# A transformer block's forward and backward pass on one core: chunks emitted as a skewed pipeline, weight-gradient matmuls interleaved, broadcasts in parts over two DMA queues

## The chip, the core and the metric

The kernel runs on 1 core of one Trainium2 chip. The metric is device time in microseconds (us). TensorE (PE, with its weight loads as PEld), VectorE (DVE), ScalarE (ACT) and GpSimd (POOL) compute; SyncE (SP) and POOL each issue DMAs. Every engine works through its own list of instructions in a fixed order and waits at the first one whose inputs or buffers are not ready.

## The reference

`reference` returns the output of one block and the gradients of a given `grad_out` with respect to seven of its inputs. S = 2048 tokens, D = 512, F = 1792, 32 heads of 16, bfloat16. The attention of a token sees 8 positions: itself and 7 earlier ones, two apart.

```python
qkv = (x @ wqkv)...                         # q, k, v: heads of 16
idx = pos[:, None] - arange(8) * 2          # a window of W = 8, dilation 2
logits = einsum("bhsd,bhswd->bhsw", q, k[idx]) * scale
o = einsum("bhsw,bhswd->bhsd", softmax(logits), v[idx]) @ wo
h  = x + attention(layernorm(x))
h2 = h + gelu(layernorm(h) @ w1 + b1) @ w2 + b2
outputs: h2, and d/d(x, wqkv, wo, w1, b1, w2, b2) of sum(h2 * grad_out)
```

## The kernel before, in words

The tokens are cut into NC = 4 chunks of CH = 512 (tiles of 128 tokens by 512 features). Channels stand on the partitions, 128 at a time (G = 4 groups). The work runs in four stages.

**Forward, chunk after chunk (the loop at L227).** Layernorm, transposes and q, k, v (`psq`, L251). For each group g DVE multiplies q by eight shifted views of k (`pr`, L260) and PE sums over a head with a small indicator matrix (`lg`, L264). Softmax on DVE and ACT gives `attn` (L269 to L279), which is transposed (`pta`, `aT`) and written to DRAM by `put_wh` (`attn_f`, `attn_b`). Then `bcast` (L145) reads 1 MB back for each group, each head's row copied to its 16 channels (`bc`, L305, on SP's queue); DVE multiplies it by the shifted v (L306) and PE sums the eight products (`pso`, L309). After that come `psh` (L317), the second layernorm, the first FFN matmul (`psf`, L333), the gelu on ACT and DVE, stores of its three intermediates to `x_d`, `s_d`, `g_d` on POOL's queue, and the second FFN matmul (`ps2`, L351).

**FFN backward, chunks 3, 2, 1, 0 (`ffn_bwd`, L423).** `psg` (L447), the gelu's derivative on DVE, `psx` (L459), and the layernorm's backward (`ln_bwd`, L409), which leaves `gh`.

**Weight gradients, in two blocks.** L566 to L582 make w2's (`psw2`, L578) from `g_d`, read back through transposing DMAs on SP's queue (`gtm`, L575). `tail_weights` (L600) makes w1's and wo's (`psw1`, L612; `pswo`, L623) from `h1tm` and `otm`, read in the same way. Both are written under `later(LOW)`, which gives them a low priority in the list that the framework orders before the run; how they then lie in each engine's order is shown below.

**Attention backward, chunks 3 to 0.** `attn_bwd1` (L468): `psgo`, the product of go and shifted v (`bp`, L489) and its sums (`ga`, L493). `attn_bwd2` (L499): the softmax's backward, `put_wh` of its result to `gl_b`, then four broadcasts of `attn_b` (`bv`, L534) and four of `gl_b` (`bg`, L539), all on POOL's queue, each multiplied on DVE (L535, L541, L542) and summed on PE (`psa`, L525), then `psy` (L552) and `ln_bwd`. After all chunks the last block makes wqkv's gradient (`psq`, L653).

What orders the work: the framework emits in the order of the program text and by priority; tiles of one tag share a number of buffers, and an instruction that needs a buffer waits for its last reader. In PSUM there are 4 accumulators of one tag (`acc`, L91), 2 for transposes and 2 for `lg` and `ga`. In SBUF `pr`/`bp` and the broadcasts share the tag `big` with 4 buffers.

Of the kernel before, what the change touches and what calls it, by code (L numbers as in the profile page):

```python
# [10 lines left out]
P = 128  # L11
# [23 lines left out]
def kernel(  # L35
# [37 lines left out]
    @contextmanager  # L73
    def later(n):
        keep = tc.cur_priority
        tc.cur_priority = keep + n
        yield
        tc.cur_priority = keep

# [7 lines left out]
    ps_acc = ctx.enter_context(tc.tile_pool(name="ps_acc", bufs=4, space=PSUM))  # L87
    ps_t = ctx.enter_context(tc.tile_pool(name="ps_t", bufs=2, space=PSUM))
    ps_l = ctx.enter_context(tc.tile_pool(name="ps_l", bufs=2, space=PSUM))

    def acc(name):  # L91
        return ps_acc.tile([P, CH], F32, name=name, tag="acc")
# [70 lines left out]

    def load_x(c):
        x = fr.tile([P, TC, D], BF16, name=f"x{c}", tag="x", bufs=2)
        sync.dma_start(out=x[:], in_=tm(xf[c * CH:(c + 1) * CH, :]))
        return x

    xs = {0: load_x(0)}
    wn = A_wqkv.rearrange("(dc p) j -> p dc j", p=P)  # L170
    for dc in range(DC):
        nat = fr.tile([P, 3 * D], BF16, name=f"nat{dc}", tag="nat", bufs=2)
# [15 lines left out]
    ptb = ps_t.tile([P, 8 * P], BF16, name="ptb", tag="pt")  # L188
    nc.tensor.transpose(ptb[:, 0:FT], b1r[:, :], ident[0:FT, 0:FT])
    nc.vector.tensor_copy(out=b1c[:], in_=ptb[:, 0:FT])  # L190
    pq.dma_start(out=w1[:], in_=B_w1.rearrange("(dc p) f -> p dc f", p=P))
# [10 lines left out]
    def layernorm(src, dst, rstd, c, nm):  # L202
        st = fl.tile([P, TC, 6], F32, name=f"st{nm}", tag="st", bufs=2)
        mv = fl.tile([P, TC, 2], F32, name=f"mv{nm}", tag="mv", bufs=2)
        ve = fl.tile([P, TC], F32, name=f"ve{nm}", tag="ve", bufs=2)
# [10 lines left out]
    def to_T(src, dst, nm):  # L216
        for d2 in range(DC // 2):
            pt = ps_t.tile([P, 8 * P], BF16, name=f"pt{nm}{d2}", tag="pt")
# [7 lines left out]
    ks, vs = {}, {}  # L226
    for c in range(NC):  # L227
        x = xs.pop(c)
        if c + 1 < NC:
            xs[c + 1] = load_x(c + 1)  # L230
        ln1 = fr.tile([P, TC, D], BF16, name=f"ln1_{c}", tag="ln1", bufs=1)
        layernorm(x, ln1, rstd1, c, f"a{c}")
        pq.dma_start(out=tm(ln1_d[c][:]), in_=ln1[:])
        ln1T = fr.tile([P, DC, CH], BF16, name=f"ln1T{c}", tag="ln1T", bufs=1)
        to_T(ln1, ln1T, f"a{c}")
# [8 lines left out]
        ks[c], vs[c] = k, v  # L244
# [37 lines left out]
        def to_wh(src, sb_pool, nm):  # L282
            t_ = sb_pool.tile([P, 2, CH], BF16, name=f"aT{nm}", tag="aT", bufs=2)
            pt = ps_t.tile([P, 8 * P], BF16, name=f"pt{nm}", tag="pt")
            for b in range(2):
                for j in range(TC):
                    nc.tensor.transpose(pt[:, (b * TC + j) * P:(b * TC + j + 1) * P], src[:, j, b * P:(b + 1) * P], ident[:])
# [401 lines left out]
```

## Time and profile before

| what | us |
|---|---|
| three runs | 1167.06, 1156.75, 1151.91 |
| median | 1156.75 |
| the profiled execution | 1156.15 |
| its span, first to last instruction | 1154.4 |
| what lies around the span | 1.75 |

The profile page gives busy time by engine, then groups of instructions by line: `x16 | 36.7, 2292 | 93.1 <-DMA` means 16 instructions, 36.7 us busy, 2292 ns for one, and 93.1 us in which their engine stood idle before them, ended by that DMA. A row of the stage view has the stretch, its length, busy us of PE, PEld, DVE, ACT and POOL with the number of instructions, then the granted clock of PE (1.00 is full), the mean busy share of the 16 DMA engines, and GB/s. DMA share times length is called DMA time below; it can pass 1.0 where packets of two queues overlap on an engine.

### The profile page before, as it was taken

Reading aid. Unit: us, or ns where it says so; the run is one execution under the profiler, and the core shown is the slowest. Engines: PE = TensorE matmul, PEld = TensorE weight load, DVE = VectorE, ACT = ScalarE, POOL = GpSimd, SP = SyncE. Lnnn points to the kernel's source line nnn. Section 1 sums busy time; section 2 is a strip of 40 time slices with the busy share of each in tenths; the row PEclk is TensorE's granted clock in tenths of the full one; section 3 lists DMA queues with packets and bytes.
Section 4 is the critical chain, followed back from the end, with each engine's and each line's share of the span. In section 5 each row is a group of like instructions: output and inputs, shape, how many; then the busy total and the mean of one; then the engine's idle time right before and its main releaser. Section 6 shows DMA issues by size and latency. Waiting matters only on the chain.

```text
span 1154.4 us, 10992 instructions
## 1 busy us (share of the span) xinstructions
PE 748.9 (65%) x4066; PEld 328.0 (28%) x4066; DVE 539.5 (47%) x790; ACT 372.0 (32%) x529; POOL 270.6 (23%) x392
## 2 busy tenths in 40 slices
PE   3357844791687275788669566199784766854668
PEld 1223421340233021233224222045332232321223
DVE  3545153543445233799998500000466675585500
ACT  4117530661284045455553011011231122221201
POOL 5205330431151125434431000200212212211100
PEclk9678876895798687887999799599996786967879
DMA  7265427444452789856543844996739668577293
GB/s 263 89 143 179 159 74 159 141 164 106 104 201 92 173 170 314 245 173 182 167 144 81 185 110 107 264 189 135 186 111 221 151 165 193 150 180 197 59 229 97
DMA packets 166516, 186.18 MB, mean 161 GB/s; under 512 B 124925, under 2 KB 138110, under 8 KB 160318
## 3 DMA queue, kind: packets, MB, share of 16 engines
q0 software_dynamic: 33792, 125.95, 38.4%
q1 hardware_dynamic: 132670, 59.53, 23.6%
q8 instruction: 32, 0.52, 0.2%
q14 instruction: 22, 0.18, 0.0%
HBM read 93.00 MB, written 63.56 MB: 136 GB/s over the span
## 4 chain that ended last, share of the span: by engine, by line
issue 24%; DVE 16%; PE 12%; DMA 10%; ACT 5%; POOL 3%; SPq 1%; POOLq 0%; ACTq 0%; DVEq 0%
PE psq L653 3%; PE psa L525 2%; DMA bg<-gl_b 2%; DMA bv<-attn_b 2%; DVE gh L449 2%; DVE bp L489 2%; DMA bc<-attn_f 2%; DVE by L441 1%; PE ps L351 1%; SPq L648 1%; ACT by L435 1%; DVE by L439 1%; ACT bu L438 1%; POOL gq_d L530 1%; DVE lua L420 1%
## 5 line engine op out<-in xcount | busy, mean ns | idle before, releaser
L541 DVE TENSOR_TENSOR bh<-bg,bk 128x4096 bf16<-128x4096 bf16 x16 | 36.7, 2292 | 194.9 <-DMA bg<-gl_b 194.9
L309 PE MATMUL pso<-bc,ident 128*128 128x512 bf16 x128 | 45.0, 516 | 92.6 <-DVE bc L306 92.6
L447 PE MATMUL psg<-goutT,w2T 128*128 128x512 bf16 x224 | 63.7, 441 | 34.4 <-DVE gb1p L449 29.3
L306 DVE TENSOR_TENSOR bc<-bc,v 128x4096 bf16<-128x4096 bf16 x16 | 36.7, 2292 | 93.1 <-DMA bc<-attn_f 93.1
L578 PE MATMUL psw<-gout,gtm 128*128 128x512 bf16 x224 | 57.4, 389 | 30.3 <-DMA gtm<-g_d 30.1
L525 PEld LDWEIGHTS <-ident 128*128 128x128 bf16 x384 | 41.8, 113 | 122.5 <-issue 40.0
L333 PE MATMUL psf<-ln2T,w 128*128 128x512 bf16 x224 | 60.7, 429 | 20.3 <-ACT u L335 18.1
L612 PE MATMUL psw<-h1tm,ln2a 128*128 128x512 bf16 (+1 forms) x256 | 50.5, 359 | 25.7 <-DMA h1tm<-gh_d 25.7
L351 PE MATMUL ps<-w,g 128*128 128x512 bf16 x224 | 55.6, 397 | 11.3 <-ACT u L335 9.7
L260 DVE TENSOR_TENSOR pr<-q,k 128x4096 bf16<-128x4096 bf16 x16 | 35.8, 2296 | 56.2 <-ACT q L253 56.2
L525 PE MATMUL psa<-bh,ident 128*128 128x512 bf16 x128 | 43.2, 499 | 28.6 <-DVE bh L541 28.6
L653 PE MATMUL psq<-gqt,ln1a 128*128 128x512 bf16 x192 | 45.2, 398 | 18.9 <-DMA ln1a<-ln_d 17.6
L525 PE MATMUL psa<-bv,ident 128*128 128x512 bf16 x128 | 39.8, 475 | 23.5 <-DVE bv L535 23.5
L530 POOL DMA_DIRECT2D gq_d<-gt x48 | 25.6, 534 | 121.2 <-ACT gt L527 76.9
L459 PE MATMUL psx<-w1T,gh 128*128 128x512 bf16 x224 | 51.5, 390 | 2.3 <-DVE gb1p L449 2.3
L535 DVE TENSOR_TENSOR bv<-bv,go 128x4224 bf16<-128x4224 bf16 x16 | 37.4, 2356 | 32.5 <-DMA bv<-attn_b 32.5
L310 ACT CAST oT<-pso 128x512 bf16<-128x512 f32 x16 | 9.4, 585 | 126.5 <-PE pso L309 126.5
L309 PEld LDWEIGHTS <-ident 128*128 128x128 bf16 x128 | 14.1, 121 | 121.4 <-DVE bc L306 102.1
L527 ACT ACTIVATE gt<-psa 128x512 bf16<-128x512 f32 x32 | 19.1, 597 | 87.6 <-PE psa L525 82.7
L251 PE MATMUL psq<-ln1T,wqkv 128*128 128x512 bf16 x192 | 44.5, 394 | 0.7 <-ACT ln1T L224 0.7
L447 PEld LDWEIGHTS <-w2T 128*128 128x128 bf16 x224 | 24.4, 109 | 71.3 <-issue 53.3
L435 ACT ACTIVATE by<-bu 128x1024 bf16<-128x1024 bf16 x28 | 29.5, 1056 | 45.7 <-DVE gb1p L449 45.7
(183 smaller groups left out, 1461.6 us busy)
## 6 DMA issues: line engine op xcount, KB each, us to landing
bv<-attn_b POOLq DMA_DIRECT2D x16, 1056.0 KB, 10.6
bg<-gl_b POOLq DMA_DIRECT2D x16, 1056.0 KB, 8.5
bc<-attn_f SPq DMA_DIRECT2D x16, 1024.0 KB, 11.2
x_d<-u POOLq DMA_DIRECT2D x28, 256.0 KB, 3.4
s_d<-s POOLq DMA_DIRECT2D x28, 256.0 KB, 3.0
g_d<-g POOLq DMA_DIRECT2D x28, 256.0 KB, 3.2
bu<-x_d POOLq DMA_DIRECT2D x28, 256.0 KB, 3.2
bs<-s_d POOLq DMA_DIRECT2D x28, 256.0 KB, 3.4
```

The costliest lines, as they stand in the source:

```text
L251: nc.tensor.matmul(ps[:], lhsT=wqkv[:, dc, jt * P:(jt + 1) * P], rhs=ln1T[:, dc, :], start=(dc == 0), stop=(dc == DC - 1))
L309: nc.tensor.matmul(ps[:], lhsT=ident[:], rhs=bc[:, w, :], start=(w == 0), stop=(w == W - 1))
L333: nc.tensor.matmul(ps[:], lhsT=w1[:, dc, ft * P:(ft + 1) * P], rhs=ln2T[:, dc, :], start=(dc == 0), stop=(dc == DC - 1))
L351: nc.tensor.matmul(ps[:], lhsT=gs[ft // 2][:, ft % 2, j * P:(j + 1) * P], rhs=w2[:, ft, :], start=(ft == 0), stop=False)
L435: nc.scalar.activation(out=y[:], in_=u[:], func=ACT.Square)
L447: nc.tensor.matmul(ps[:], lhsT=w2T[:, dc, ft * P:(ft + 1) * P], rhs=gT[:, dc, :], start=(dc == 0), stop=(dc == DC - 1))
L459: nc.tensor.matmul(ps[:], lhsT=gh1[ft // 2][:, ft % 2, j * P:(j + 1) * P], rhs=w1T[:, ft, :], start=(ft == 0), stop=(ft == FT - 1))
L525: nc.tensor.matmul(ps[:], lhsT=ident[:], rhs=src[:, w, o:o + CH], start=(w == 0), stop=(w == W - 1))
L535: nc.vector.tensor_tensor(out=bc[:], in0=bc[:], in1=over_w(gos[c][:, g, :], HB), op=ALU.mult)
L578: nc.tensor.matmul(ps[:], lhsT=gtm[:, t // TC, t % TC, :], rhs=gout[t // TC][:, t % TC, :], start=(t == 0), stop=(t == NT - 1))
L612: nc.tensor.matmul(ps[:, 0:nf * P], lhsT=ln2a[:, t // TC, t % TC, dc * P:(dc + 1) * P], rhs=tmx[:, t // TC, t % TC, 0:nf * P], start=(t == ...
L653: nc.tensor.matmul(ps[:], lhsT=ln1a[:, t // TC, t % TC, dc * P:(dc + 1) * P], rhs=gqt[:, t // TC, t % TC, :], start=(t == order[0]), stop= ...
```

## The change

The same operations on the same tiles are written in another order, with other buffers. Nothing is left out and no operand changes shape, but for the broadcasts, which are cut along the window.

- **Forward:** the loop's body becomes `f_qkv`, `f_attn`, `f_o`, `f_h`, `f_ffn`. Chunk c+1's `f_attn` is written ahead of chunk c's `f_o`, and chunk c+2's `f_qkv` behind chunk c's `f_ffn`. The transposes of wqkv and wo (`f_wT`) move from the end of chunk 0 to the start.
- **Broadcasts:** `bcast` cuts each into parts: two halves on SP and POOL for `bc` (512 KB each) and `bg` (528 KB each), four quarters of 264 KB, all on POOL, for `bv`.
- **FFN backward:** in the order 0, 3, 2, 1. w2's gradient becomes a generator of 14 pieces (one for each ft); from the second chunk on, `ffn_bwd` takes one piece after every second pair of ft and one at its end.
- **Attention backward:** `attn_bwd1` and `attn_bwd2` become `b_ga`, `b_sm`, `b_gv`, `b_gqk`, `b_gx`. Chunk c-1's `b_ga` and `b_sm` are written ahead of chunk c's `b_gqk`; w1's and wo's gradients become a generator of 20 pieces taken between them.
- **Buffers:** PSUM has 2 accumulators `accA` and 2 `accB` (FFN and weight gradients) in place of 4 shared ones, and one transpose buffer each for `ptA` and `ptB` in place of 2 shared. `big` becomes `pr` with 2 buffers and `bc` with 3.

```diff
-    ps_acc = ctx.enter_context(tc.tile_pool(name="ps_acc", bufs=4, space=PSUM))
-    ps_t = ctx.enter_context(tc.tile_pool(name="ps_t", bufs=2, space=PSUM))
+    psum = ctx.enter_context(tc.tile_pool(name="psum", bufs=2, space=PSUM))
+    def acc(name, tag="accA"):
+        return psum.tile([P, CH], F32, name=name, tag=tag)
+    def ptile(name, tag="ptA"):
+        return psum.tile([P, 8 * P], BF16, name=name, tag=tag, bufs=1)
...
+    def bcast(out_t, d_t, g, n, parts):
+        wq = W // len(parts)
+        for i, e in enumerate(parts):
+            b = d_t[8 * g:8 * g + 8, i * wq * n:(i + 1) * wq * n]
+            e.dma_start(out=out_t[:, i * wq:(i + 1) * wq, :].rearrange("p w t -> p (w t)"),
+                        in_=_ap(b, [[0, DH], [W * n, 8], [1, wq * n]]))
...
-            bc = fr.tile([P, W, CH], BF16, name=f"bc{c}_{g}", tag="big", bufs=4)
-            sync.dma_start(out=bc[:].rearrange("p w t -> p (w t)"), in_=bcast(attn_f[c], g, W * CH))
+            bc = fr.tile([P, W, CH], BF16, name=f"bc{c}_{g}", tag="bc", bufs=3)
+            bcast(bc, attn_f[c], g, CH, (sync, pq))
...
+    f_qkv(0)
+    f_attn(0)
+    f_qkv(1)
+    f_wT()
+    for c in range(NC):
+        if c + 1 < NC:
+            f_attn(c + 1)
+        f_o(c)
+        f_h(c)
+        f_ffn(c)
+        if c + 2 < NC:
+            load_x(c + 2)
+            f_qkv(c + 2)
...
+            if f2 % 2 == 1:
+                take(filler, 1)
...
+    gw2 = gw2_gen()
+    none = iter(())
+    for i in range(NC):
+        ffn_bwd(i, none if i == 0 else gw2)
+    take(gw2, FT)
...
+            bcast(bc, attn_b[c], g, HB, (pq, pq, pq, pq))
...
+            bcast(bc, gl_b[c], g, HB, (sync, pq))
...
+    wg = weights_gen()
+    b_ga(3)
+    b_sm(3)
+    b_gv(3)
+    for c in (3, 2, 1, 0):
+        take(wg, 2)
+        if c > 0:
+            b_ga(c - 1)
+            b_sm(c - 1)
+        b_gqk(c, bp)
+        take(wg, 1)
+        b_gx(c, bp, wqkvT)
+        take(wg, 1)
+        if c > 0:
+            b_gv(c - 1)
+            take(wg, 1)
+    take(wg, 100)
```

**How it moves instructions.** A name such as `bc1_0` is chunk 1, group 0; the number behind it is a buffer's.

DVE in the forward pass before, from chunk 1's softmax (`mx`, `sm`, `e`, `attn`) on:

```order
L269 TENSOR_REDUCE mx1_1_1232<-lg1_1_1086 128x64
L278 RECIPROCAL sm1_0_1228<-sm1_0_1228 128x64
L271 TENSOR_TENSOR e1_1_1234<-lg1_1_1086,mx1_1_1232 128x512
L279 TENSOR_TENSOR attn1_92<-e1_0_1225,sm1_0_1228 128x512
L277 TENSOR_REDUCE sm1_1_1237<-e1_1_1234 128x64
L278 RECIPROCAL sm1_1_1237<-sm1_1_1237 128x64
L279 TENSOR_TENSOR attn1_92<-e1_1_1234,sm1_1_1237 128x512
L306 TENSOR_TENSOR bc1_0_1259<-bc1_0_1259,v1_1007 128x4096
L306 TENSOR_TENSOR bc1_1_1273<-bc1_1_1273,v1_1007 128x4096
L306 TENSOR_TENSOR bc1_2_1287<-bc1_2_1287,v1_1007 128x4096
L306 TENSOR_TENSOR bc1_3_1301<-bc1_3_1301,v1_1007 128x4096
L207 BN_STATS stb1_1345<-h1_1315 128x6
```

The same engine now, where it comes to chunk 0's broadcasts:

```order
L317 TENSOR_TENSOR bc0_0_877<-bc0_0_877,v0_231 128x4096
L284 TENSOR_TENSOR pr1_0_705<-q1_527,k1_528 128x4096
L284 TENSOR_TENSOR pr1_1_739<-q1_527,k1_528 128x4096
L317 TENSOR_TENSOR bc0_1_892<-bc0_1_892,v0_231 128x4096
L284 TENSOR_TENSOR pr1_2_773<-q1_527,k1_528 128x4096
L284 TENSOR_TENSOR pr1_3_807<-q1_527,k1_528 128x4096
L317 TENSOR_TENSOR bc0_2_907<-bc0_2_907,v0_231 128x4096
L293 TENSOR_REDUCE mx1_0_841<-lg1_0_703 128x64
L317 TENSOR_TENSOR bc0_3_922<-bc0_3_922,v0_231 128x4096
```

Before, a chunk's broadcasts come right behind its own softmax, which they read; now chunk 1's products stand between chunk 0's broadcasts.

ACT at the end of FFN backward before (`jkf` and `luf` belong to `ln_bwd`, `go3` to the attention's backward, `ow2` holds a piece of w2's gradient):

```order
L419 ACTIVATE luf3_4150<-bln20_4048,c2f3_4148 128x512
L481 CAST go3_4175<-psgo3_2_4189 128x512
L481 CAST go3_4175<-psgo3_3_4195 128x512
L570 CAST gb2_4358<-psb2_4341 1x512
L581 CAST ow20_4383<-psw20_4366 128x512
L581 CAST ow21_4408<-psw21_4391 128x512
```

Now, in chunk 3's FFN backward (`by` and `bu` are its derivative):

```order
L462 CAST ow20_3391<-psw20_3374 128x512
L482 ACTIVATE by3_2_3398<-bu3_2_3394 128x1024
L482 ACTIVATE by3_3_3424<-bu3_3_3420 128x1024
L485 ACTIVATE bu3_2_3394<-bs3_2_3395,one_t_72 128x1024
L485 ACTIVATE bu3_3_3420<-bs3_3_3421,one_t_72 128x1024
L462 CAST ow21_3468<-psw21_3451 128x512
L482 ACTIVATE by3_4_3475<-bu3_4_3471 128x1024
```

w2's gradient, which stood behind all of FFN backward, now lies between its chunks' derivatives.

DVE in the attention's backward before, where chunk 3's second set of broadcasts begins (`sp`, `gl`: the softmax's backward):

```order
L507 TENSOR_TENSOR sp3_1_5166<-ga3_1_4204,rs3_1_5168 128x512
L508 TENSOR_TENSOR gl3_5159<-attn3_94,sp3_0_5160 128x512
L508 TENSOR_TENSOR gl3_5159<-attn3_94,sp3_1_5166 128x512
L541 TENSOR_TENSOR bh3_0_5252<-bg3_0_5250,bk3_5187 128x8x512
L542 TENSOR_TENSOR bg3_0_5250<-bg3_0_5250,bq3_5189 128x4224
```

The same place now:

```order
L553 TENSOR_TENSOR bp2_2_5002<-go2_4904,bv2_4906 128x4096
L553 TENSOR_TENSOR bp2_3_5036<-go2_4904,bv2_4906 128x4096
L609 TENSOR_TENSOR bh3_0_5107<-bg3_0_5104,bk3_5098 128x4096
L568 TENSOR_TENSOR sp2_0_5071<-ga2_0_4932,attn2_87 128x512
L568 TENSOR_TENSOR sp2_1_5077<-ga2_1_4933,attn2_87 128x512
```

Before, `bh3_0`, whose broadcast reads what `gl3` leads to, came right behind `gl3`; now chunk 2's `bp` stands ahead of it.

More of the change, by code (lines that the diff above doesn't have):

```diff
@@ L1 @@
[L1 removed]
+from contextlib import ExitStack
 import numpy as np
@@ new lines, in f_wT @@
+    def f_wT():
+        for src, dst, nb in ((wqkv, wqkvT_d, NJ), (wo, woT_d, DC)):
+            for db in range(0, nb, 2):
+                pt = ptile(f"ptw{nb}_{db}", "ptB")
+                st_ = fr.tile([P, 2, D], BF16, name=f"wT{nb}_{db}", tag="wqT", bufs=1)
+                for i in range(2):
+                    for dc in range(DC):
+                        o = (i * DC + dc) * P
+                        nc.tensor.transpose(pt[:, o:o + P], src[:, dc, (db + i) * P:(db + i + 1) * P], ident[:])
+                nc.scalar.copy(out=st_[:], in_=pt[:].rearrange("p (b d) -> p b d", b=2))
+                pq.dma_start(out=dst[db * P:(db + 2) * P, :].rearrange("(b p) d -> p b d", p=P), in_=st_[:])
```

380 lines of the change are left out of this document (180 added, 200 removed).

## The prediction

> **What bounds the kernel now.** I first read the busy times, to see whether one engine sets the end.
>
> ```profile
> span 1154.4 us, 10992 instructions
> PE 748.9 (65%) x4066; PEld 328.0 (28%) x4066; DVE 539.5 (47%) x790; ACT 372.0 (32%) x529; POOL 270.6 (23%) x392
> ```
>
> None does: PE, the fullest, idles for a third of the span. So I cut the span where the work changes (first `psg` matmul at 469, last `psx` at 621, last `psw2` at 719, last `psy` at 1079) and asked for each stage who is full there. In these rows follow the length: busy PE, PEld, DVE, ACT, POOL, then PE's granted clock, DMA share, GB/s.
>
> ```profile
> 0.00:469.00 469.00, 271.05 (x1619) 121.67 (x1620) 194.75 (x288) 194.60 (x257) 141.48 (x192) 0.79 0.58 160
> 475.00:621.00 146.00, 112.82 (x455) 46.88 (x455) 135.26 (x310) 79.90 (x100) 55.13 (x77) 0.89 0.51 159
> 621.00:719.00 98.00, 67.55 (x394) 25.34 (x392) 27.52 (x27) 12.47 (x23) 3.73 (x7) 0.93 0.58 132
> 719.00:1079.00 360.00, 242.10 (x1368) 110.36 (x1364) 170.97 (x140) 72.20 (x127) 65.72 (x111) 0.81 0.73 174
> 1079.00:1154.40 75.40, 52.91 (x228) 22.70 (x226) 8.86 (x20) 12.79 (x24) 3.03 (x4) 0.86 0.62 140
> ```
>
> Only FFN backward has a full engine (DVE, 135 of 146 us). The forward pass, w2's gradient, and the attention's backward with the other gradients have none above 69%. There the order of the work is the bound: everything of one chunk waits for that chunk's broadcasts. The waits say so; the columns are total, times, longest.
>
> ```profile
> DVE bh L541 <- DMA bg<-gl_b: 194.9, 14, 161.9
> DVE bc L306 <- DMA bc<-attn_f: 93.1, 16, 16.7
> DVE bv L535 <- DMA bv<-attn_b: 32.5, 10, 7.4
> PE psw L578 <- DMA gtm<-g_d: 30.1, 36, 13.2
> ```
>
> The 161.9 is DVE standing still while PE makes the weight gradients alone, 621 to 813. One forward chunk, on PE, shows the 93.1:
>
> ```profile
> 247.91 10.52 PE L251 MATMUL psq<-ln1T,wqkv 128*128 128x512 bf16 x48
> 288.44 3.60 PE L309 MATMUL pso<-bc,ident 128*128 128x512 bf16 x8 [17.18 <-DVE bc L306]
> 302.30 2.45 PE L309 MATMUL pso<-bc,ident 128*128 128x512 bf16 x8 [2.65 <-DVE bc L306]
> 316.97 9.69 PE L333 MATMUL psf<-ln2T,w 128*128 128x512 bf16 x36 [0.57 <-ACT ln2T L224]
> 336.80 10.04 PE L351 MATMUL ps<-w,g 128*128 128x512 bf16 x44 [1.44 <-ACT u L335]
> 351.82 10.52 PE L251 MATMUL psq<-ln1T,wqkv 128*128 128x512 bf16 x48
> ```
>
> From one `psq` to the next are 103.9 us, and PE idles 17.2 of them for the first broadcast and some more for each of the next.
>
> **The change, stage by stage.** The instructions stay, so each stage's new time lies between its fullest resource and the old time, and I work out where.
>
> *Forward, now until chunk 0's `psg` ends.* The period of a chunk comes from the rows above. (a) `psf` to the end of `ps2` is 351.8 - 317.0 = 34.8 us, paced by ACT:
>
> ```profile
> 318.00:346.00 28.00, 23.55 (x112) 10.25 (x110) 13.10 (x24) 24.92 (x31) 14.55 (x21) 0.95 0.59 201
> L253 ACT CAST k<-psq 128x512 bf16<-128x512 f32 x16 | 9.2, 586 | 6.7 <-PE psq L251 6.7
> L306 DVE TENSOR_TENSOR bc<-bc,v 128x4096 bf16<-128x4096 bf16 x16 | 36.7, 2292 | 93.1 <-DMA bc<-attn_f 93.1
> L260 DVE TENSOR_TENSOR pr<-q,k 128x4096 bf16<-128x4096 bf16 x16 | 35.8, 2296 | 56.2 <-ACT q L253 56.2
> ```
>
> Chunk c+2's q, k, v now lie in it: their 12 evictions add 12 x 0.59 = 7 us to ACT, so 42. DVE has 15 us free there, room for most of the seven 2.3 us products (three `bc`, four `pr`) that its order now puts there. The next rows are issues of the broadcasts: count, size, median us to landing.
>
> ```profile
> bv<-attn_b POOLq DMA_DIRECT2D x16, 1056.0 KB, 10.6
> bg<-gl_b POOLq DMA_DIRECT2D x16, 1056.0 KB, 8.5
> bc<-attn_f SPq DMA_DIRECT2D x16, 1024.0 KB, 11.2
> ```
>
> (b) The `lg` and `pso` matmuls follow. Three buffers hold three broadcasts and the fourth waits for the first `pso`; then it needs its landing (11.2 us median now, two halves at once), less what PE has to do meanwhile, its product and 8 matmuls: 14 us. (c) `psh` to `psf` is 317.0 - 304.8 = 12.2 us; the softmax of the next chunk on DVE and the single transpose buffer add some 5: 17. The sum is 73. The fullest engine bounds it from below at 64.7 (PE busy in one chunk), the old period from above at 103.9. I take 76, near the sum, since nothing on that path is new but the two-queue DMAs.
>
> ```profile
> 247.90:351.80 103.90, 64.68 (x389) 28.56 (x388) 45.95 (x65) 44.45 (x61) 28.93 (x38) 0.79 0.47 135
> 92.54 9.27 PE L333 MATMUL psf<-ln2T,w 128*128 128x512 bf16 x36 [0.57 <-ACT ln2T L224]
> ```
>
> Chunk 0's `psf` starts at 92.5 now. Ahead of it come chunk 1's `psq` (10.5) and 64 transposes of weights, most of it in PE's idle time before the first `pso`: 100. Two periods bring chunk 2's `psf` to 252; its chunk has no `psq` and no `lg` beside it, so chunk 3's starts some 52 later (34.8 + 17), at 304. Then FFN 3 and chunk 0's FFN backward share DVE: 13.1 + 135.3 / 4 = 47, with losses 52. The stage ends at 356. It held 469 + 146 / 4 = 505.5 before: **-149**.
>
> *FFN backward of three chunks with w2's gradient, until the last `psx`.* PE has 632 matmuls of 512 columns (4 x 56 `psx`, 3 x 56 `psg`, 224 `psw2`, 16 `psb2`). At full clock one takes 20 / 94 = 0.213 us:
>
> ```profile
> 1120.00:1140.00 20.00, 20.00 (x94) 9.11 (x93) 0.00 (x0) 3.28 (x6) 0.00 (x0) 1.00 0.77 176
> 654.40 5.16 SPq L575 DMA_TRANSPOSE gtm<-g_d  x4
> 660.22 5.17 SPq L575 DMA_TRANSPOSE gtm<-g_d  x4
> ```
>
> That is 135 us, and PE becomes the bound here; DVE needs 3 x 34 = 101, and SP, which issues the transposing reads of one ft every 5.8 us, 14 x 5.8 = 81, now hidden. PE and DVE hand each pair of accumulators back and forth, and there are two where there were four: I take 85% of PE, 158 us. Before: 146 x 3 / 4 + 98 = 207.5. **-49**.
>
> *Attention's backward with w1's and wo's gradients.* The gradients' PE time goes under the broadcasts, and the wait of 161.9 goes. So does this gap, in which PE has nothing until w1's inputs are loaded; chunk 3's `psgo`, `ga` and first `psa` now lie in it:
>
> ```profile
> 743.65 1.86 PE L612 MATMUL psw<-h1tm,ln2a 128*128 128x512 bf16 x4 [22.71 <-DMA h1tm<-gh_d]
> ```
>
> What bounds it next is the DMA engines, since w1's and wo's transposing reads and all 32 broadcasts of 1 MB now fall into one stretch. DMA time there is 0.73 x 360 = 263 us, PE 242, DVE 171 (with the 27.5 that were done in the stage before, some 200). The longest stretches at a high share are these:
>
> ```profile
> 745.00:813.00 68.00, 62.63 (x315) 30.50 (x314) 0.00 (x0) 10.85 (x20) 0.36 (x1) 0.98 0.80 156
> 430.00:470.00 40.00, 25.20 (x90) 8.75 (x90) 16.19 (x28) 21.18 (x27) 22.85 (x32) 0.83 1.14 292
> 284.00:300.00 16.00, 9.09 (x24) 2.78 (x24) 6.93 (x4) 1.48 (x3) 1.08 (x2) 0.60 0.99 222
> ```
>
> At a share of 0.84, a little above the longest, it takes 312. **-48**. The range runs from 277 (share 0.95) to 360. The last chunk still has no partner to overlap with.
>
> *The tail* (last `ln_bwd`, the reload of ln1, wqkv's gradient) is the same code: 75.4.
>
> *At nothing.* Splitting a broadcast: the row of 284 to 300 has SP's single queue filling the 16 engines (0.99), so halves on two queues finish no sooner together. POOL issues 64 parts more than before, 48 of them for `bv`:
>
> ```profile
> L534 POOL DMA_DIRECT2D bv<-attn_b x16 | 8.6, 538 | 26.1 <-PE ga L493 26.1
> ```
>
> At 0.54 us that is 35 us on an engine that is 23% busy; without that cover each of the 48 broadcasts would start 0.7 us later. The 16 parts added on SP lie between its transposing reads.
>
> Sum of the span: 356 + 158 + 312 + 75 = 901. With 1.75 around it: 903 us. This is against the profiled execution, 1156.15, which stands 0.6 below the median of the runs.
>
> **The rivals.**
>
> *DMA stays at the share it has* in the attention's backward, 0.73, because each broadcast still waits for a buffer and a queue. DMA time of the whole is 0.62 x 1154.4 = 716, of which 47 lie in the tail: 669 / 0.73 + 75 = 992, so 994. For it: bursts at 0.99 were always followed by gaps. Against it: the three-deep buffers are asked for a chunk ahead now.
>
> *The overlap is better:* a share of 0.95 in all stages but the tail. Forward (0.58 x 469 + 0.51 x 36.5) / 0.95 = 306, FFN backward at PE's 135 / 0.95 = 142, attention's 277, tail 75: 802. For it: 1.14 over 40 us above. Against it: that stretch had no broadcasts.
>
> *POOL's issues held back.* 96 broadcast parts come from POOL, 32 did. If each waited for the end of a running DVE product, the 64 more would cost at most 64 x 2.29 = 147: 1050. Its sign would be longer issues where DVE is full. These two rows are of issues in the stages with DVE at 42% (`x_d`) and 93% (`bs`):
>
> ```profile
> L347 POOL DMA_DIRECT2D x_d<-u x28 | 19.9, 713 | 10.3 <-ACT u L335 9.8
> L433 POOL DMA_DIRECT2D bs<-s_d x28 | 19.9, 712 | 21.3 <-DVE by L441 8.1 <-DVE c2f L417 7.0 <-PE psf L333 6.1
> ```
>
> They are equal, so I give it little. The Trainium skill, SBUF — State Buffer, section "SBUF: two separate sides", says that a DMA issued from GpSimd cannot have its descriptors written while DVE runs in a mode that takes the port the two share. By that rule this rival would be the forecast; the trace does not show it for the products used here.
>
> *Slower: DVE in order behind late broadcasts.* DVE's new order puts `bc` products between an FFN's `z` and `g`, and `bh` between `bp` and `sp`. A broadcast that lands late now stops the FFN too, and with it ACT, PE and the stores. If every one of the 48 is waited for in full, they cost their landings as listed above: 16 x (10.6 + 8.5 + 11.2) = 485 us, stretched by the denser DMA (share 0.80 for 0.62) to 626. With DVE's 539.5 busy and the tail's 66.5 without DVE that makes 1232. It turns slower than 1157 + 23 from 12 us a broadcast on.
>
> *The gain is given back:* the order moves as shown, but the two accumulators and the single transpose buffer make each stage wait as long as before: 1155.
>
> **How the numbers follow.** Forecast 903: 0.60. DMA at 0.73, 994: 0.20. Better overlap, 802: 0.11. POOL held back, 1050: 0.03. Given back, 1155: 0.03. Slower, 1232: 0.03. About 2% is what a measurement can tell from no change. Faster by more than that: 0.94, within it 0.03, slower 0.03. The range of 8 in 10 takes in the 994 and half of the way to 802: 835 to 1010.
>
> **What would show it.** In the profile after: `psf` of successive chunks some 76 us apart; DVE's wait for `bg` far below 194.9, with no single wait above 20; `psw` matmuls between `psg`; a DMA share near 0.8 over the span and PE's granted clock above 0.82, with less PE busy time for the same matmuls. The stages should end near 356, 514 and 826. The prediction is wrong if the forward period stays above 90, if the first `psw1` still waits 20 us for `h1tm`, or if the DMA share stays at 0.65 while broadcasts are waited for.

## The result and the profile after

| | before | after |
|---|---|---|
| runs | 1151.91 to 1167.06 | 1016.42, 1025.60, 1027.08 |
| median, us | 1156.75 | 1025.60 |
| ratio, 95% interval | | 0.883, 0.871 to 0.895 |
| the profiled execution; its span | 1156.15; 1154.4 | 1027.08; 1025.3 |

The change gains 131 us where 253 were forecast; the time lies above the range. The times and ratios of the experiments below are those of the runs within 1.5% of each kernel's fastest, so that e6, whose 987.1 over all its runs is quoted in an expectation, stands at 979.3. The busy times of after:

```profile
span 1025.3 us, 11102 instructions
PE 723.7 (71%) x3999; PEld 328.7 (32%) x4066; DVE 537.0 (52%) x790; ACT 371.3 (36%) x527; POOL 302.4 (29%) x456
```

No engine is full, as before. The stage view of after, cut where the prediction cut (end of chunk 0's `psg`, last `psx`, last chunk's first `psy`, end); columns as there:

```profile
0.00:440.00 440.00, 284.65 (x1651) 131.04 (x1676) 209.82 (x333) 201.67 (x263) 150.43 (x220) 0.82 0.70 177
440.00:604.00 164.00, 145.11 (x637) 62.43 (x648) 121.78 (x276) 79.38 (x107) 55.81 (x80) 0.96 0.85 214
604.00:948.00 344.00, 240.57 (x1489) 112.28 (x1514) 196.20 (x162) 77.25 (x134) 93.19 (x152) 0.83 0.82 181
948.00:1025.30 77.30, 53.37 (x227) 22.99 (x230) 9.21 (x20) 13.04 (x24) 3.01 (x4) 0.87 0.63 138
```

The stages were forecast at 356, 158, 312 and 75. So 84 of the missing 124 us of span lie ahead of 440, 32 in the attention's backward, 6 in FFN backward and 2 in the tail. The waits show what the change did reach (total, times, longest):

```profile
DVE bv L595 <- DMA bv<-attn_b: 63.6, 10, 17.6
DVE bc L317 <- DMA bc<-attn_f: 63.5, 8, 15.0
DVE bh L609 <- DMA bg<-gl_b: 35.7, 7, 12.5
PE psg L494 <- DMA goutT<-in_grad_out_dram: 19.7, 1, 19.7
```

The wait for `bg`, 194.9 with one of 161.9, is 35.7 with none above 12.5; that for `bc` went from 93.1 to 63.5, but in 8 pieces of up to 15.0 in place of 16; that for `bv` has doubled, from 32.5.

**The forward pass.** First `psf` matmul of each chunk on PE:

```profile
110.62 1.03 PE L350 MATMUL psf<-ln2T,w 128*128 128x512 bf16 x4
198.74 1.24 PE L350 MATMUL psf<-ln2T,w 128*128 128x512 bf16 x4
283.75 7.52 PE L350 MATMUL psf<-ln2T,w 128*128 128x512 bf16 x23 [0.22 <-issue]
348.70 5.67 PE L350 MATMUL psf<-ln2T,w 128*128 128x512 bf16 x15
```

The periods are 88.1, 85.0 and 65.0, where 76, 76 and 52 were forecast, and the first comes 10.6 late. Inside chunk 0's FFN, right behind its first `psf`, three engines stand still one behind the other:

```profile
123.34 2.29 DVE L317 TENSOR_TENSOR bc<-bc,v 128x4096 bf16<-128x4096 bf16 x1 [13.04 <-DMA bc<-attn_f]
128.81 1.06 ACT L358 ACTIVATE s<-z 128x1024 bf16<-128x1024 bf16 x1 [8.76 <-DVE z L356]
130.39 1.87 PE L274 MATMUL psq<-ln1T,wqkv 128*128 128x512 bf16 x4 [9.21 <-ACT k L276]
```

DVE's next instruction is chunk 1's `bc`, whose broadcast has not landed. Chunk 0's `z`, which is ready, is queued behind it; ACT's `s` needs `z`, and PE needs the accumulator that ACT empties behind `s`. The wait is 13.0 us here, 15.0 in the next chunk and 7.5 in the third.

**The border of forward and backward.** A stretch of the stage view, a wait of PE, SP's queue, and two more waits:

```profile
348.70:439.80 91.10, 47.67 (x175) 18.41 (x178) 36.28 (x76) 37.10 (x44) 30.57 (x43) 0.75 1.19 178
374.05 1.01 PE L494 MATMUL psg<-goutT,w2T 128*128 128x512 bf16 x2 [19.67 <-DMA goutT<-in_grad_out_dram]
364.30 31.18 SPq L427 DMA_TRANSPOSE w1T<-in_B_w_dram  x1
402.76 1.27 ACT L352 ACTIVATE u<-psf,b1c 128x512 bf16<-128x512 f32 x2 [13.40 <-DMA x_d<-u]
403.50 3.57 PE L350 MATMUL psf<-ln2T,w 128*128 128x512 bf16 x8 [15.92 <-ACT u L352]
```

Chunk 3's FFN and chunk 0's FFN backward take 91 us, with PE busy for 48. PE's list puts chunk 0's `psg` among chunk 3's `psf`, and PE stands still for 19.7 us until `goutT`, a transposing read, has landed. `w1T`, the next such read, holds SP for 31.2 us. Before, it held it for 8.6:

```profile
432.98 8.64 SPq L401 DMA_TRANSPOSE w1T<-in_B_w_dram  x1
```

Meanwhile a store of `x_d` does not finish, `u` has no free buffer, and ACT and PE stop. The last two columns are worth a look: the DMA share is 1.19 and only 178 GB/s move. The page of before and that of after, on the packets' time:

```profile
q0 software_dynamic: 33792, 125.95, 38.4%
q1 hardware_dynamic: 132670, 59.53, 23.6%
```

```profile
q0 software_dynamic: 38912, 125.69, 43.4%
q1 hardware_dynamic: 134974, 59.79, 32.4%
```

The same 186 MB took 0.62 x 1154.4 = 716 us of DMA time before and 0.76 x 1025.3 = 780 after. The increase is nearly all in q1, the queue of SP: 0.236 x 1154.4 = 272 us before, 0.324 x 1025.3 = 332 after. POOL's q0 took 443 and 445.

**The attention's backward.** The transposing reads of w1's inputs, first a row of before, then two of after:

```profile
h1tm<-gh_d SPq DMA_TRANSPOSE x16, 5.2
```

```profile
h1tm<-gh_d SPq DMA_TRANSPOSE x16, 19.0
610.14 48.94 SPq L643 DMA_TRANSPOSE h1tm<-gh_d  x8
```

They land in 19.0 us in place of 5.2 (medians of the three and the four reads whose landing the traces show). All 16 held SP for 85 us, where they held it for 56 before.

### The profile page after: what moved, and what is told of

The parts are those of the page before. It is cut to its first block, busy times and chain, and to the rows that moved or that the text cites. A ratio compares the mean times of both kernels' runs of the same rounds, so it can differ in the third digit from the quotient of the medians.

```text
span 1025.3 us, 11102 instructions
## 1 busy us (share of the span) xinstructions
PE 723.7 (71%) x3999; PEld 328.7 (32%) x4066; DVE 537.0 (52%) x790; ACT 371.3 (36%) x527; POOL 302.4 (29%) x456
## 4 chain that ended last, share of the span: by engine, by line
PE 15%; DMA 13%; issue 9%; DVE 7%; SPq 5%; POOL 4%; ACT 3%; POOLq 0%; DVEq 0%; ACTq 0%
DMA bv<-attn_b 6%; DMA bg<-gl_b 4%; PE psq L697 4%; PE psa L582 3%; SPq L643 2%; PE psx L508 2%; PE psw L647 2%; PE psy L622 2%; SPq L693 1%; POOL bv L239 1%; DVE bh L609 1%; SPq L655 1%; DVE bv L595 1%; DMA bs<-s_d 1%; PE psgo L547 1%
## 5 line engine op out<-in xcount | busy, mean ns | idle before, releaser
L582 PEld LDWEIGHTS <-ident 128*128 128x128 bf16 x384 | 39.9, 107 | 142.4 <-DVE bv L595 45.3
L350 PE MATMUL psf<-ln2T,w 128*128 128x512 bf16 x218 | 64.9, 445 | 24.2 <-ACT u L352 23.5
L317 DVE TENSOR_TENSOR bc<-bc,v 128x4096 bf16<-128x4096 bf16 x16 | 36.6, 2288 | 63.5 <-DMA bc<-attn_f 63.5
L494 PE MATMUL psg<-goutT,w2T 128*128 128x512 bf16 x218 | 53.8, 382 | 21.2 <-DMA goutT<-in_grad_out_dram 19.7
L274 PE MATMUL psq<-ln1T,wqkv 128*128 128x512 bf16 x188 | 50.1, 410 | 18.3 <-ACT k L276 17.0
L582 PE MATMUL psa<-bh,ident 128*128 128x512 bf16 x123 | 37.0, 445 | 31.1 <-DVE bh L609 30.5
L622 PE MATMUL psy<-wqkvT,gt 128*128 128x512 bf16 x188 | 47.9, 412 | 14.8 <-DVE lua L443 14.3
L239 POOL DMA_DIRECT2D bv<-attn_b x64 | 33.9, 538 | 80.5 <-PE psa L582 76.3
L320 PE MATMUL pso<-bc,ident 128*128 128x512 bf16 x122 | 38.4, 459 | 24.8 <-DVE bc L317 24.3
L609 DVE TENSOR_TENSOR bh<-bg,bk 128x4096 bf16<-128x4096 bf16 x16 | 36.4, 2288 | 35.7 <-DMA bg<-gl_b 35.7
L352 ACT ACTIVATE u<-psf,b1c 128x512 bf16<-128x512 f32 x56 | 36.5, 683 | 36.3 <-PE psf L350 19.4
L350 PEld LDWEIGHTS <-w 128*128 128x128 bf16 x224 | 24.8, 112 | 70.1 <-issue 53.8
```

Source lines behind the costliest of these rows:

```text
L274: nc.tensor.matmul(ps[:], lhsT=wqkv[:, dc, jt * P:(jt + 1) * P], rhs=ln1T[:, dc, :], start=(dc == 0), stop=(dc == DC - 1))
L350: nc.tensor.matmul(ps[:], lhsT=w1[:, dc, ft * P:(ft + 1) * P], rhs=ln2T[:, dc, :], start=(dc == 0), stop=(dc == DC - 1))
L494: nc.tensor.matmul(ps[:], lhsT=w2T[:, dc, ft * P:(ft + 1) * P], rhs=gT[:, dc, :], start=(dc == 0), stop=(dc == DC - 1))
L582: nc.tensor.matmul(ps[:], lhsT=ident[:], rhs=src[:, w, o:o + CH], start=(w == 0), stop=(w == W - 1))
L609: nc.vector.tensor_tensor(out=pr[:], in0=bc[:, :, 0:CH], in1=back_w(k[:, g, PAD:HB], CH), op=ALU.mult)
L622: nc.tensor.matmul(ps[:], lhsT=gts[c][sel][:, g, j * P:(j + 1) * P], rhs=wqkvT[:, sel * G + g, :], start=(n == 0), stop=(n == NJ - 1))
```

## The experiments

Theory A when the result was seen: DVE's order holds the forward pass, and transposing reads mixed with other traffic hold the border and the attention. The rivals were the split of the broadcasts, the number of buffers and the two accumulators. A stage with transposing reads differs by 10 us and more between kernels that issue it alike, so the verdicts go by the runs where they can. In each kernel the cuts are as above; line numbers differ a little.

**e1: broadcasts whole.**

```diff
-            bcast(bc, attn_f[c], g, CH, (sync, pq))
+            bcast(bc, attn_f[c], g, CH, (sync,))
-            bcast(bc, attn_b[c], g, HB, (pq, pq, pq, pq))
+            bcast(bc, attn_b[c], g, HB, (pq,))
-            bcast(bc, gl_b[c], g, HB, (sync, pq))
+            bcast(bc, gl_b[c], g, HB, (pq,))
```

> The changed kernel with its broadcasts whole again: bc on SP's queue, bv and bg on POOL's, as before the change. Theory A (the missing time lies in the order of the work, not in the split): the split was costed at nothing, so the time stays within 10 us of 1025.6, and the stage borders of the changed kernel (110.6 first psf, 439.7 end of chunk 0's FFN backward, 604 last psx, 948 last psy) move by less than 6 us each. Theory B (the split costs: parts on POOL's queue delay the stores, and bg's halves on SP's queue lie behind the transposing reads of h1tm, eight of which held SP for 48.9 us): at least 20 us faster, most of it in the attention's backward, 604 to 948, with bg's landing back near 8.5 us from 10.5 and 12.6, and x_d's back near 3.4 from 9.0.

Measured 983.2 us, 0.852 of before (0.842 to 0.861): 42 faster than the change. Theory A missed here; a split priced at nothing was wrong in this surrounding. The forward and border end at 419.3 for 439.8, the attention's backward takes 333.7 for 344 (the profiled execution is 14 us above the time given). `x_d` lands in 4.8 for 9.0, but `bg` in 11.2, not 8.5.

**e4: only the forward's broadcasts whole.**

```diff
-            bcast(bc, attn_f[c], g, CH, (sync, pq))
+            bcast(bc, attn_f[c], g, CH, (sync,))
```

> The changed kernel with only the forward's broadcasts bc whole on SP's queue; bv and bg stay in parts. Theory A (the split costs nothing): forward borders within 4 us, the time within 6 us of 1025.6. Theory B (halves on POOL's queue stand ahead of the stores of x_d, s_d and g_d and delay u's buffers): x_d lands in 3 to 4 us in place of 9.0, ACT's wait for u's buffer goes, and the three forward periods are some 5 us shorter each: about 1010.

Measured 1030.3 us (0.892, 0.883 to 0.901). Theory B's 1010 did not come, though `x_d` lands in 4.8. Inconclusive as a whole, plainer by its stage: the forward and border end 15 us earlier, at 424.4, and the time is lost again behind it (FFN backward 171 for 164, the attention 357 for 344), where the program is the same. Chunk 1's first `bc` product, in e4:

```profile
118.21 2.29 DVE L317 TENSOR_TENSOR bc<-bc,v 128x4096 bf16<-128x4096 bf16 x1 [5.49 <-DMA bc<-attn_f]
```

The first `psf` is at 110.2 in e4 and 110.6 in the change, but the first broadcast is there 5 us sooner, and DVE waits 5.5 for 13.0. In the change the six halves of three broadcasts are under way together, and the second and third product then follow without a wait; whole ones come one by one, and the first comes early. This is read from the rows; no run tests it alone. The third period of e4 is 57.6 us, from these two rows:

```profile
271.82 2.43 PE L350 MATMUL psf<-ln2T,w 128*128 128x512 bf16 x7 [0.22 <-issue]
329.46 2.84 PE L350 MATMUL psf<-ln2T,w 128*128 128x512 bf16 x8
```

**e2: DVE's order.** Chunk c+1's `bc` products are put behind chunk c's last gelu product.

```diff
+            last_g[c] = nc.vector.tensor_tensor(out=gt[:], ...)
...
+            with tc.issue_after(last_g[c - 1].ins) if c > 0 else nullcontext():
                 nc.vector.tensor_tensor(out=bc[:], in0=bc[:], in1=back_w(v[:, g, PAD:HB], CH), op=ALU.mult)
```

> The changed kernel, with one thing more: on DVE the four bc products of chunk c+1 are put behind the last gelu product g of chunk c's FFN; other engines' lists may follow. Theory A (DVE in order behind late broadcasts): bc of chunk 1 holds DVE 13.0 us in the middle of chunk 0's FFN (110.3 to 123.3), and with it ACT 8.8 and PE 9.2; likewise in chunks 1 and 2. Without it the forward period falls from 88.1 and 85.0 to about 77, and the whole by 3 x 8 = 24 us, to about 1002. Theory B (the forward pass is held by the broadcasts themselves: three buffers, the fourth asked for late): the stall moves to pso behind the FFN, the period stays above 84 and the time within 8 us of 1025.6.

Measured 999.8 us (0.867, 0.859 to 0.874): 26 faster, where theory A had 24. PE, then DVE, of e2:

```profile
187.69 1.03 PE L351 MATMUL psf<-ln2T,w 128*128 128x512 bf16 x4
263.29 8.00 PE L351 MATMUL psf<-ln2T,w 128*128 128x512 bf16 x24
145.65 6.69 DVE L318 TENSOR_TENSOR bc<-bc,v 128x4096 bf16<-128x4096 bf16 x3
```

The first `psf` is at 111.6, so the periods are 76.1 and 75.6: the 76 of the prediction. They give 21 us; in the profile the border is 11 us shorter too, and differences of 7 us and less elsewhere go both ways. The three products now follow one another without a wait.

**e3: the transposing reads made plain.** The reads of `w2T`, `goutT`, `w1T`, `h1tm` and `otm` move the same bytes without turning them.

```diff
+    def plain(t_, src):
+        n = t_.shape[-1]
+        m = t_.shape[1]
+        sync.dma_start(out=t_, in_=_ap(src[0:1, 0:1], [[m * n, P], [n, m], [1, n]]))
-    sync.dma_start_transpose(out=w2T[:], in_=B_w2[:, :])
+    plain(w2T[:], B_w2)
...
-                sync.dma_start_transpose(out=tmx[:, c, :, 0:nf * P], in_=gh1_d[c][f0 * P:(f0 + nf) * P, :])
+                plain(tmx[:, c, :, 0:nf * P], gh1_d[c][f0 * P:(f0 + nf) * P, :])
```

> The changed kernel with the transposing reads of w2T, goutT, w1T (at the border of forward and backward) and of h1tm and otm (attention's backward) made plain reads of the same bytes in the same place; their transposition is left out, so the backward's values are not the reference's. The two stages are told apart by their borders. Theory A (the transposing reads, mixed with stores and broadcasts, hold up the other transfers: w1T took 31 us on SP, and a store of x_d was then waited for 13.4 us by ACT and 15.9 by PE): from 348.7, chunk 3's first psf, to 439.7, the end of chunk 0's FFN backward, 91 us fall to about 55, and the attention's backward from 344 to about 315; in all some 60 us, 965. Theory B (the border and the attention are held by the order of the work and the number of buffers): each stage falls by less than 10 us, the whole stays above 1005.

Measured 933.6 us (0.809, 0.802 to 0.817): 92 faster, more than theory A's 60. The border and the attention in e3, and `h1tm`:

```profile
351.10:410.20 59.10, 43.59 (x176) 17.45 (x178) 36.97 (x78) 39.58 (x47) 32.84 (x47) 0.91 1.03 303
561.40:861.40 300.00, 232.34 (x1490) 109.68 (x1514) 196.49 (x163) 77.38 (x134) 93.31 (x152) 0.90 0.73 208
h1tm<-gh_d SPq DMA_DIRECT2D x12, 512.0 KB, 10.3
```

The border takes 59 us for 91, at 303 GB/s for 178; the attention's backward 300 for 344, at a lower share (0.73 for 0.82) and more GB/s (208 for 181). The Trainium skill, Advanced Engine Details and Errata, section "X-Bar Transpose (TRN2)", says that such reads are as fast as regular ones. Beside broadcasts the traces differ: the transposing reads of `h1tm` landed in 19.0 us (median of three), plain ones in their place in 10.3 (of two).

**e6: the border without transposing reads, by a correct way.** Broadcasts whole; e2's order for chunks 1 and 2; `goutT`, w1 and w2 turned on PE.

```diff
-            sync.dma_start_transpose(out=goutT[c][:], in_=gof[c * CH:(c + 1) * CH, :])
+            to_T(gout[c], goutT[c], f"o{c}", "ptA")
...
+            (f_w1T, f_w2T)[c]()
...
-    sync.dma_start_transpose(out=w1T[:], in_=B_w1[:, :])
+    sync.dma_start(out=w1T[:], in_=w1T_d[:, :].rearrange("(ft p) d -> p ft d", p=P))
```

> Four edits to the changed kernel together, to see whether the costs found add up: broadcasts whole (as in e1); chunk 1's and 2's bc products behind the FFN ahead of them on DVE (as in e2, chunk 3's left free); goutT made by 16 PE transposes and two ACT copies a chunk from gout in place of transposing reads; w1's and w2's transposes made on PE in chunks 0 and 1 of the forward pass, stored to DRAM and read back plainly. Theory A (the border of forward and backward is held by transposing reads): chunk 3's psf starts near 317 (107 + 76 + 76 + 58), chunk 0's FFN backward ends 59 later, at 376, as with plain reads in e3; then 165 + 332 + 79 as in e1: about 950. Theory B (it is held by any large load there, 6 MB in all): the border stays above 85 us, and the time above 975.

Measured 979.3 us (0.846, 0.841 to 0.851), not theory A's 950. Border and attention of e6, and its SP queue:

```profile
323.20:386.60 63.40, 52.31 (x232) 21.58 (x230) 39.55 (x82) 43.74 (x53) 33.78 (x48) 0.89 1.07 282
542.70:913.60 370.90, 241.76 (x1517) 112.98 (x1515) 196.99 (x163) 77.25 (x134) 71.90 (x114) 0.83 0.94 172
614.40 51.86 SPq L670 DMA_TRANSPOSE h1tm<-gh_d  x3
```

The border came nearly as theory A had it (63 us long for the expected 59, ending at 386.6 for 376), which speaks against theory B's 85. But the attention's backward, the same program as in e1, took 371 us in place of 334, with three reads of `h1tm` holding SP for 51.9 (the profiled execution is 13 us above the time given). What the border gave was lost there.

**e11: SP's order.** The stores of `gx` and of w1's and wo's gradients go from SP's to ACT's queue, in e6.

```diff
-            sync.dma_start(out=out1f[t * P:(t + 1) * P, :], in_=gx[:])
+            nc.scalar.dma_start(out=out1f[t * P:(t + 1) * P, :], in_=gx[:])
```

> e6 (987.1, attention's backward 369 us of it) with one thing moved: the stores of gx and of w1's and wo's gradients are issued by ACT in place of SP, so that in the attention's backward nothing but transposing reads lies on SP's queue. Theory A (SP's list in order: a store of gx behind three reads that hold SP 51.9 us keeps its buffer, then DVE, ACT and PE wait in turn, 46.7 us for c2a and 40.3 for lua): the stage falls to about 315, the whole to about 935. Theory B (the reads and the broadcasts hold each other up on the DMA engines, whatever stands on SP): the stage stays above 345, the whole above 960.

Measured 991.8 us (0.855, 0.846 to 0.864): theory B. The attention of e11, SP's queue in it, and a wait of that queue:

```profile
558.60:915.00 356.40, 242.84 (x1517) 112.80 (x1516) 197.52 (x163) 76.93 (x134) 70.37 (x114) 0.83 0.94 179
565.30 178.86 SPq L670 DMA_TRANSPOSE h1tm<-gh_d  x16
SPq L670 <- PE psw L674: 30.9, 1, 30.9
```

The stage takes 356 us, not 315. With nothing between them the 16 reads still take 178.9 us from the first to the last. In 41 of these SP issues none and waits, mostly for a buffer that PE's `psw` frees; in the other 138 the reads hold it, 8.6 us each, where those of before held it for 3.5. It is not the queue's order that holds them.

**e7: `h1tm` and `otm` turned on PE,** on top of e6.

```diff
-                sync.dma_start_transpose(out=tmx[:, c, :, 0:nf * P], in_=gh1_d[c][f0 * P:(f0 + nf) * P, :])
+                turned(tmx[:, c, :, 0:nf * P], gh1_d[c][f0 * P:(f0 + nf) * P, :], nf, f"h{f0}_{c}")
...
+    def turned(dst, src, nf, nm):
+        hp = bp.tile([P, 4, CH], BF16, name=f"hp{nm}", tag="hp", bufs=2)
+        sync.dma_start(out=hp[:, 0:nf, :], in_=src.rearrange("(i p) t -> p i t", p=P))
+        for t2 in range(0, TC, 2):
+            pt = ptile(f"ptx{nm}_{t2}", "ptB")
...
+                    nc.tensor.transpose(pt[:, o:o + P], hp[:, i, (t2 + j) * P:(t2 + j + 1) * P], ident[:])
+            nc.scalar.copy(out=dst[:, t2:t2 + 2, :], in_=pt[:, 0:2 * nf * P].rearrange("p (j f) -> p j f", j=2))
```

> e6 and one thing more: h1tm and otm are read plainly and turned on PE (288 transposes of 128x128, 36 copies by ACT), with one buffer tmx in place of two. Theory A (the transposing reads of h1tm and otm, mixed with broadcasts, cost the attention's backward its 44 us): from 332 the stage falls to some 300, the whole to about 920. Theory B (PE becomes the bound: 288 x 0.11 = 32 us more on the 240 it has there, and its list puts them between psa): the stage stays above 325, the whole above 943.

Measured 920.6 us (0.796, 0.793 to 0.799): 59 faster than e6, and the best kernel here. Its border, FFN backward and attention:

```profile
324.30:389.60 65.30, 52.62 (x232) 22.03 (x230) 39.78 (x83) 43.66 (x53) 34.16 (x48) 0.89 1.08 280
389.60:540.30 150.70, 138.56 (x653) 61.42 (x652) 119.28 (x268) 78.30 (x105) 46.39 (x65) 1.00 0.81 192
540.30:840.60 300.30, 248.95 (x1793) 127.35 (x1791) 196.69 (x163) 111.45 (x173) 74.05 (x114) 0.93 0.81 213
```

The attention takes 300 us though PE does 288 transposes more. All runs lie between 918.5 and 922.7; those of e6 between 976.7 and 998.4.

**e14: the same edit on the change alone,** with its split, its forward pass and its border.

> The changed kernel with one edit: h1tm and otm read plainly and turned on PE (288 transposes, 36 copies by ACT, one buffer tmx). Split, forward pass and border as in the change. Theory A (the transposing reads of h1tm and otm cost the attention's backward what it lacks): the stage falls from 342 to about 300, the whole from 1025.6 to about 985, and the runs lie closer together. Theory B (e7's gain over e6 came from their interplay with whole broadcasts only): the stage stays above 325, the whole above 1010.

Measured 988.0 us (0.852, 0.843 to 0.860): theory A within 3 us for the whole, 10 above it for the stage.

```profile
604.50:914.50 310.00, 255.17 (x1799) 128.46 (x1797) 196.83 (x163) 111.46 (x173) 93.19 (x153) 0.91 0.73 206
```

The attention's backward is 310 for 344, against the 312 of the prediction. The runs lie between 982.5 and 993.8, no closer than the change's three (1016.4 to 1027.1), so that part of the expectation was not met. `w2T`, `goutT` and `w1T` are still transposing reads here, but e3, where they are not, spreads over 18 us too.

**e12: e7 with the broadcasts split again.**

```diff
-            bcast(bc, gl_b[c], g, HB, (pq,))
+            bcast(bc, gl_b[c], g, HB, (sync, pq))
```

(and `bc` and `bv` likewise, the reverse of e1)

> e7 (920.6) with the broadcasts cut into parts again as in the change: halves on SP and POOL for bc and bg, quarters on POOL for bv. No transposing read is left in the attention's backward. Theory A (the split cost only where SP's queue and the engines were full of transposing reads): within 8 us of 920.6. Theory B (parts cost by themselves, by more issues and smaller pieces): 15 us or more slower. Theory C (two queues bring a broadcast in sooner once nothing stands in their way): 10 us or more faster.

Measured 927.9 us (0.802, 0.796 to 0.807), 7 slower than e7, within theory A's 8; the intervals overlap, though no run of e12 is as fast as one of e7. The split does not speed a broadcast up even on a free SP queue: the halves of `bg` land in 9.2 and 10.1 us, a whole one of e7 in 10.2. This is what the Trainium skill says in DMA: Bandwidth & Descriptors, section "Issuing engines are not separate DMA queues": transfers that several engines start interleave on the same DMA engines.

**e13: four buffers for `bv` and `bg`,** in e7.

```diff
-            bc = bl.tile([P, W, HB], BF16, name=f"bv{c}_{g}", tag="bc", bufs=3)
+            bc = bl.tile([P, W, HB], BF16, name=f"bv{c}_{g}", tag="bc", bufs=4)
```

(`goutT` and `ow2` give up their second buffer for it)

> e7 with four buffers in place of three for bv and bg (goutT and ow2 have one in place of two for it). Theory A (in the attention's backward POOL waits 41.6 us for a buffer before it can ask for the next bv, and DVE then waits 37.3 for bv and 24.1 for bg: three buffers are the bound now): the stage falls from 298 to about 270, the whole to about 895; FFN backward may lose up to 5. Theory B (the engines' own work and the DMA engines, at a share of 0.8, are): within 8 us of 920.6.

Measured 939.1 us (0.811, 0.804 to 0.816): slower by 18, so neither theory's time came. The attention took 309 for 300, so three buffers are not its bound. The rest lies in FFN backward, 167 us from the first `psx` to the last for 151, where `goutT` and `ow2` have one buffer.

**e9: the forward pass without the skew.**

```diff
-        if c + 1 < NC:
-            f_attn(c + 1)
...
+        f_qkv(c)
+        f_attn(c)
         f_o(c)
         f_h(c)
         f_ffn(c)
...
```

> The changed kernel with the forward's loop written chunk after chunk again (f_qkv, f_attn, f_o, f_h, f_ffn of one chunk, f_wT behind chunk 0); buffers, split and backward as in the change. Theory A (the skew shortened the period from 103.9 to 86): the forward's periods go back to about 100, chunk 0's FFN backward ends some 3 x 16 = 48 us later, about 1070. Theory B (the framework overlaps chunks by readiness in any case, so the text's order matters little): within 12 us of 1025.6.

Measured 1046.6 us (0.904, 0.896 to 0.913): 21 slower, between theory A's 1070 and theory B's bound of 1038. The periods are 108.6, 91.9 and 90.3, about the 100 of theory A: the skew is worth 20, 7 and 25 us, although it puts late broadcasts into the FFN. Part of that comes back elsewhere: the first `psf` is at 98.6, 12 us sooner than in the change, and FFN backward and the attention, whose text is the same, take 150 for 164 and 339 for 344:

```profile
470.90:620.90 150.00, 142.34 (x650) 61.66 (x650) 119.87 (x272) 75.75 (x103) 52.69 (x76) 1.00 0.87 214
620.90:960.00 339.10, 234.41 (x1516) 109.68 (x1514) 196.43 (x163) 77.28 (x134) 93.06 (x152) 0.86 0.81 184
```

**e10: four accumulators of one tag.**

```diff
-        return psum.tile([P, CH], F32, name=name, tag=tag)
+        return psum.tile([P, CH], F32, name=name, tag="acc", bufs=4)
```

> The changed kernel with its four accumulators in one tag again, shared by all stages, in place of two and two; accumulators are then given out in the order of the text, so PE no longer mixes the q, k, v of a later chunk or the weight gradients in single matmuls between others. Theory A (two and two cost nothing, 85% of PE in FFN backward was right): within 10 us of 1025.6. Theory B (two accumulators hold up each pair of engines): FFN backward falls from 164 us toward PE's 135, the whole by 20 or more. Theory C (the split into two tags is what lets PE fill its idle time): the forward's periods go above 95 and the whole above 1045.

Measured 1033.2 us (0.893, 0.885 to 0.900), 8 slower, with an interval that overlaps the change's: theory A. The periods of 83, 85 and 70 us speak against theory C. Theory B's gain in the whole did not come. By stages it is less plain: the last `psx` ends at 585 for 604, but 48 of w2's matmuls lie behind it, and the last chunk's `psy` begins no sooner (949 for 946). Whether two and two hold up FFN backward stays open.

## Why the prediction was off

The direction and the reasons for the gain held, and its three marks of being wrong did not appear: the period stayed below 90, if barely, the share rose to 0.76, and the first `psw1` no longer waits:

```profile
L647 PE MATMUL psw<-h1tm,ln2a 128*128 128x512 bf16 (+1 forms) x249 | 53.8, 355 | 0.5 <-issue 0.2
```

PE's clock rose to 0.85 and its busy time fell, as said, though a part of that fall is 67 matmuls that the trace of after lacks (3999 records for 4066). None of the marks stood on the border or on the attention's DMA time; of the signs, the 76 us and the ends of the stages did not come.

1. **Forward, -149 forecast, -66 measured (505.5 to 439.8).** Of the 84 us, 10.6 lie ahead of the first `psf`: the prediction put most of chunk 1's `psq` and the weights' transposes into PE's idle time, and e9, which has them and chunk 1's softmax later, starts at 98.6. Another 21 are the two periods of 88 and 85: the step "I take 76, near the sum, since nothing on that path is new but the two-queue DMAs". New was DVE's order too. The rival "DVE in order behind late broadcasts" is this mechanism, priced at the landing of all 48 broadcasts and at 0.03. It came true in its small form, one wait a chunk, of 13.0, 15.0 and 7.5 us: e2 took it away and got 76.1 and 75.6, although its products lie behind the FFN and not in it, as the sum of the prediction had them. Another 13 are the third period, 65 for 52; whole broadcasts made it 57.6 in e4.
2. **The border, 52 forecast, 91 measured.** This failed most. "FFN 3 and chunk 0's FFN backward share DVE: 13.1 + 135.3 / 4 = 47, with losses 52" has no term for `w2T`, `goutT` and `w1T`, nor for PE's list, in which `psg` waits for `goutT` ahead of chunk 3's remaining `psf`. e3 and e6 brought the border to 59 and 63.
3. **FFN backward, 158 forecast, 164 measured.** Right: PE is busy for 145 of 164 us, 88%, and `psw2` lies between `psg`. The same text took 150 us in e9 and 171 in e4.
4. **Attention's backward, 312 forecast, 344 measured.** The step "DMA time there is 0.73 x 360 = 263 us" took that time as fixed. At a share of 0.82, close to the 0.84 taken, it was 0.82 x 344 = 282, for the same bytes (174 x 360 and 181 x 344 are both 62 to 63 MB). It is no amount of work but the time that packets take, and the packets of the transposing reads took longer here (the numbers are in the last section). e14 and e7, without these reads, gave 310 and 300. That e14's 310 is so near the 312 of the prediction is luck: its share is 0.73 and its DMA time 0.73 x 310 = 226. The rival "DMA stays at the share it has" fell, and its time was nearer for another reason.
5. **"Splitting a broadcast: at nothing".** Without transposing reads in the attention it costs 7 us (e12 against e7); in the change up to 42 (e1), part of it by a later first broadcast (e4) and the order that follows. How e1's 42 divide is not settled, since a stage with transposing reads moves by nearly as much between kernels: the attention's backward with the same text took 338 (e2), 339 (e9), 344 (the change) and 357 us (e4), and with whole broadcasts 334 (e1) and 371 (e6).
6. **Rivals.** POOL's issues were not held back: the 64 parts of `bv` take as long as the 16 whole ones did, and no trace here shows the port rule that the prediction cites. That this rival "would be the forecast" by that rule went too far: no run shows that the products used here run in the mode that the rule is for.

```profile
L239 POOL DMA_DIRECT2D bv<-attn_b x64 | 33.9, 538 | 80.5 <-PE psa L582 76.3 <-DMA bv<-attn_b 2.5 <-DMA bg<-gl_b 1.1
```

The accumulators did not cost the whole anything that e10 shows. The tail took 77.3 for 75.4.

The prediction listed the share of 1.14 at 430 to 470 for its rival of a better overlap. That stretch too held transposing reads, of `w1T`, `goutT` and `gtm`, and it moved 292 GB/s; the border of the change has a share of 1.19 and moves 178. So a share above 1 tells neither of room nor of trouble until the GB/s are read beside it. Why these reads passed there and held up the border here stays open.

## What to carry to other kernels

A DMA share times a length is not an amount that can be moved into a shorter stage: read the GB/s beside it, and where the share is high and GB/s are low, find which transfers spoil each other before filling that stage further. When a software pipeline puts another chunk's late input into an in-order engine's list, ask what stands ready behind it; here one ordering edge was worth 26 us. Transposes that PE can do in its idle time may be cheaper than transposing reads among large transfers.

## What the runs showed of the hardware

- Transposing reads move in small packets, and these take longer beside other traffic. In the attention's backward, before and in the change, SP's queue has some 38,000 packets of under 300 bytes (9.4 MB, so 250 bytes each); with the reads turned on PE (e14, e7) some 1,000 are left. Such a packet took 22 ns on average at 745 to 813 of before, with hardly anything beside it, 34 in the change's attention, 47 in that of e6 and 55 in the change's border.
- They slow the broadcasts less: POOL's packets of 600 bytes and more took 253 ns in the attention of the change and 227 in that of e14, 415 in e6 and 372 in e7, so some 10% less without the transposing reads.
- Between e6 and e7 the reads' 288 blocks went to PE, whose transposes and ACT's copies are extra work, and the attention's backward fell from 371 to 300 us at a lower DMA share (0.94 to 0.81) and with more GB/s (172 to 213); the kernels' times differ by 59.
- The spread of all runs was 22 us in e6 and 4 in e7 and e12, but 18 in e3, which has none of these reads either; what makes it is not shown.
- Of three broadcasts cut into halves on two queues the first lands 13 us behind the first `psf` and the others are there when DVE asks; whole on one queue the first is there 5 us sooner, and DVE, which works in order, needs the first.
